# Half chunks: k transposed whole, k^T v on four tiles, the middle state on VectorE, and a table of places for every attention step

## The chip, the cores and the metric

The kernel runs on one core of one Trainium2 chip. The metric is the device time of one execution in microseconds (us), from the first instruction to the last; runs of this kernel lay between 716.03 and 719.46 us, with a median of 718.99 us. The engines are named as in the profile: PE (TensorE matmul), PEld (its weight loads), DVE (VectorE), ACT (ScalarE), POOL (GpSimd), SP (the queue that issues most DMAs). Each engine works through its own instructions in order and waits on semaphores for the others.

## The reference, cut to what matters

A gated linear attention feeds two blocks of dense layers. The change is in the attention part alone, in how it is computed for three of the four batches, and in where its steps stand.

```python
B, H, S, D = 4, 8, 768, 48
f = 1.0 / (1.0 + np.exp(-f_logit))
for t in range(S):
    state = f[:, :, t, :, None] * state + np.einsum('bhd,bhe->bhde', k[:, :, t], v[:, :, t])
    y[:, :, t] = np.einsum('bhd,bhde->bhe', q[:, :, t], state)
# then, with x = y as [B, S, 384]:
h = xt @ U @ V;  u = x + h.T;  x1 = u + relu(u @ w_ch1) @ w_ch2        # d_model 384 -> 1536 -> 384
theta = x1 @ w_theta;  y = w_tok_r @ (x1 cos) + w_tok_i @ (x1 sin);  u = x1 + y;  out = u + relu(u @ w_ch)
```

## The kernel before, in words

The sequence of a batch is cut into six chunks of 128 positions. Within a chunk the gate products p (a running product of f along the chunk) are divided out: q is multiplied by p, k by 1/p, so that scores, states and outputs become matmuls. The eight heads are packed as four pairs (index j); a pair's two heads lie on partitions 0 to 47 and 64 to 111, so that one tile row of the array (64 partitions) holds one head.

For batch 0 (`start`) a chunk is worked whole: `sc` (scores), `kt` (k transposed with four whole transposes of 112x128), `kv` (k^T v, the chunk's part of the state), `xx` (output), `xt` (output transposed). For batches 1 to 3 a chunk is worked as two halves of 64 positions, with matmuls of 64x64 tiles of the array:

- `pre_a`, `pre_s`, `pre_r` (lines 237 to 266): sigmoid on ACT, the running product as a scan on DVE, q times p on POOL, then for each pair a reciprocal on DVE, and for every second pair the product k/p on POOL.
- `kt4` (376): k transposed, as 16 matmuls of one head and one half against an identity; the results of both halves stand under each other by head, and ACT copies the bank to `ktok`.
- `sc4` (355): the scores of both halves, 16 matmuls into bank A5; `mask4` (368) multiplies them by a triangle on DVE.
- `kv4` (390): k^T v of each half, 16 matmuls (`L400`), into one bank (A3 or A4 for batches 2 and 3, B1 for batch 1). Head a of a pair takes tile row a and tile column a, so two of the four tiles are in use. ACT copies both halves' results to `kvs` (`L403`); POOL adds the old state to the first half's (`L405`: the middle state), adds that to the second half's (`L407`) and multiplies by the chunk's whole product (`L408`).
- `xx4` (412): the output, 16 matmuls of masked scores with v (`L423`), then of q with the old and the middle state (`L429`), into banks B0 and B1; ACT copies both banks to `xf`.
- `xt` (345): the output of a chunk transposed by three whole transposes of 128x128.

v is loaded by `load_v` (219): for the half chunks each half of the 128 rows is copied to both halves of the partitions, so that each head finds either half of v on its own partitions.

The attention of batch b+1 is interleaved with the first dense block of batch b, `moe1(b)` (625). `moe1` is a list of 48 steps of equal weight: `w1g` (nine matmuls of 128x384, `L639`; ACT makes hh (`L644`), DVE makes hl from the same bank (`L645`)) and `w2g` (six matmuls with hh, `L656`, three with hl, `L659`), in the order w1g 0, w1g 1, w2g 0, w1g 2, w2g 1 and so on. After the last w2g of a row of them DVE adds three accumulators to xT (`L664`). `hT` (597) is one matmul, an add to xT on DVE (`L601`), a copy on ACT and a difference on POOL; three of them stand at the start of each `moe1`.

What sets the order: `place` (147) walks the list of `moe1`'s steps and puts each timed step ahead of the `moe1` step whose middle lies at or behind its time (a share of the list). `spread` gives a list of steps evenly spaced times in an interval. Before the change the attention of batches 2 and 3 is one list (`elif b > 1`, 517) spread over 0 to 0.86 of `moe1`, after its first six steps stood in the end of the `moe1` before (`NPRE`); `opening` (kt4 and sc4 of chunk 0) comes early, and `one(c)` (446) does xt of the chunk before, kv4, kt4 and sc4 of the next chunk, and xx4, all in a row. Batch 1 has its own list (543), stretched by the knots `AKNOT`. `WPOS` holds the times of four steps for each piece of the weights of `moe1` (load, scale on ACT, join on DVE `L1001` and `L1004`, split on ACT and POOL `L164`); these stand in batch 0's attention and in `moe1(0)`.

PSUM has eight banks: A0 to A2 hold w2g's accumulators, A3 and A4 take w1g in turn, A5 the scores, B0 and B1 are shared by kt4, kv4 of batch 1, xx4, xt and hT.

## Time and profile before

| | |
|---|---|
| three runs | 718.99 us median, 716.03 to 719.46 |
| the profiled execution | 717.67 us, of which the span of its instructions is 715.9 us |
| mean granted TensorE clock | 0.991 |
| busy: PE, DVE, ACT, POOL | 692.7, 385.7, 334.4, 301.1 us (97, 54, 47, 42% of the span) |
| batch 0's attention (PE waits often) | about 0 to 67 us |
| moe1(0), moe1(1), moe1(2), with the attention of batches 1, 2, 3 | about 67 to 184, 184 to 290, 290 to 394 us |
| moe1(3), then the second dense block | about 394 to 500, 500 to 716 us |

A group of the trace gives the line, the engine, the operation, the tiles it writes and reads, the shape, and then busy time and the mean length of one instruction. Matmuls overlap in the array: a 128x384 matmul is shown some 340 ns long, but the next one starts about 173 ns later, so lengths of matmuls don't add up, and what a row of them costs is read from where it starts to where the next row starts. One `mm` call on 32-bit floats stands in the trace as two instructions, a whole transpose as one.

### The profile page before, as it was taken

The numbers are of one execution on the slowest core, as the hardware profiler recorded it, in microseconds if no ns is written. First come the engines' busy times: TensorE is split into PE (matmuls) and PEld (weight loads), VectorE is DVE, ScalarE is ACT, GpSimd is POOL, SyncE is SP. The second block draws the span as 40 slices with busy tenths as digits, with TensorE's granted clock in tenths as the row PEclk, the third lists the DMA queues.
The fourth block names the chain that finished last, engine by engine and source line by source line (L and its number), as shares of the span: only waits on it lengthen the run. The fifth ranks groups of instructions, "written<-read, shape, count | busy, mean of one in ns | idle before, by whom it ended". The sixth has DMA issues, their size and how long they took to land.

```text
span 715.9 us, 15690 instructions
## 1 busy us (share of the span) xinstructions
PE 692.7 (97%) x6601; PEld 660.9 (92%) x6601; DVE 385.7 (54%) x593; ACT 334.4 (47%) x706; POOL 301.1 (42%) x320
## 2 busy tenths in 40 slices
...
GB/s 174 247 229 180 45 105 96 64 60 102 1 56 58 57 86 82 2 57 57 58 23 1 85 117 131 118 125 89 1 1 23 33 12 12 45 12 12 33 23 71
DMA packets 20606, 49.85 MB, mean 70 GB/s; under 512 B 2576, under 2 KB 11152, under 8 KB 20528
## 3 DMA queue, kind: packets, MB, share of 16 engines
...
q8 instruction: 54, 0.88, 0.6%
q10 hardware_dynamic: 192, 0.59, 0.4%
...
## 4 chain that ended last, share of the span: by engine, by line
PE 75%; DVE 9%; ACT 6%; POOL 3%; DMA 3%; issue 3%; POOLq 0%; DVEq 0%; ACTq 0%
PE ps_A L788 17%; PE ps_A L639 17%; PE ps_A L656 11%; PE ps_A L659 5%; PE ps_B L816 5%; PE ps_B L735 4%; PE ps_B L384 2%; PE ps_A L364 2%; DMA r<-in_wtok_dram 2%; DVE f L261 2%; PE ps_A L400 2%; PE ps_B L429 1%; PE ps_B L423 1%; DVE w L1004 1%; PE ps_B L574 1%
## 5 line engine op out<-in xcount | busy, mean ns | idle before, releaser
L645 DVE SCALAR_TENSOR_TENSOR hl<-ps_A,hh 128x384 fp32r<-128x384 f32 x96 | 53.0, 553 | 160.0 <-ACT hh L644 159.5
L788 PE MATMUL ps_A<-W,zh 128*128 128x384 f32 x576 | 125.1, 338 | 0.0
L639 PE MATMUL ps_A<-uh,W 128*128 128x384 f32 x576 | 119.4, 341 | 0.9 <-ACT uh L605 0.9
L656 PE MATMUL ps_A<-hh,W 128*128 128x384 f32 x552 | 115.4, 338 | 1.6 <-DVE xT L664 0.9
L644 ACT ACTIVATE hh<-ps_A 128x384 fp32r<-128x384 f32 x96 | 46.9, 488 | 133.5 <-PE ps_A L639 132.8
L639 PEld LDWEIGHTS ps_A<-uh,W 128*128 128x128 f32 x576 | 100.9, 189 | 2.9 <-ACT uh L605 1.7
L788 PEld LDWEIGHTS ps_A<-W,zh 128*128 128x128 f32 x576 | 100.7, 188 | 0.0
L656 PEld LDWEIGHTS ps_A<-hh,W 128*128 128x128 f32 x552 | 96.3, 188 | 4.0 <-DVE xT L664 1.8
L164 POOL TENSOR_TENSOR zl<-z,zh 128x768 fp32r<-128x768 f32 x24 | 44.7, 1864 | 98.1 <-ACT zh L765 53.5
L261 DVE RECIPROCAL f<-p 112x128 f32<-112x128 f32 x96 | 85.3, 923 | 0.8
L788 PE MATMUL ps_A<-W,zl 128*128 128x384 f32 x288 | 73.3, 335 | 0.0
L659 PE MATMUL ps_A<-hl,W 128*128 128x384 f32 x276 | 66.1, 338 | 2.3 <-DVE hl L645 2.3
L639 PE MATMUL ps_A<-ul,W 128*128 128x384 f32 x288 | 66.3, 336 | 0.3 <-POOL ul L164 0.2
L164 POOL TENSOR_TENSOR ul<-xT,uh 128x384 fp32r<-128x384 f32 x45 | 45.8, 1035 | 48.9 <-ACT uh L605 32.9
L264 POOL TENSOR_TENSOR raw<-raw,f 112x256 f32<-112x256 f32 x48 | 38.1, 794 | 59.4 <-DVE f L261 59.2
L639 PEld LDWEIGHTS ps_A<-ul,W 128*128 128x128 f32 x288 | 51.5, 188 | 1.2 <-DVE ul L164 0.6
L659 PEld LDWEIGHTS ps_A<-hl,W 128*128 128x128 f32 x276 | 49.7, 189 | 2.8 <-DVE hl L645 2.7
L788 PEld LDWEIGHTS ps_A<-W,zl 128*128 128x128 f32 x288 | 52.1, 188 | 0.0
L254 POOL TENSOR_TENSOR raw<-raw,p 112x512 f32<-112x512 f32 x24 | 30.8, 1285 | 45.9 <-DVE p L250 29.6
L741 DVE SCALAR_TENSOR_TENSOR ps_B<-kk,ps_B 128x384 f32<-128x384 f32 x24 | 13.5, 562 | 60.0 <-ACT kk L740 60.0
L164 POOL TENSOR_TENSOR W<-r,W 128x384 fp32r<-128x384 f32 x24 | 27.0, 1136 | 40.1 <-ACT W L167 40.1
L574 PE MATMUL ps_B<-wz 128*128 128x384 f32 x104 | 29.5, 404 | 3.9 <-POOL wz L849 3.5
...
## 6 DMA issues: line engine op xcount, KB each, us to landing
...
```

Of the source, the lines that this page charges most:

```text
L164: eng.tensor_tensor(out=out_, in0=a, in1=b, op=ALU.subtract)
L254: nc.gpsimd.tensor_tensor(out=x, in0=x, in1=p, op=ALU.mult)
L261: nc.vector.reciprocal(out=f[:, j], in_=p[:, j])
L264: nc.gpsimd.tensor_tensor(out=x, in0=x, in1=f[:, j - 1:j + 1], op=ALU.mult)
L574: mm(out=o, lhsT=t[:, 0:128], rhs=t, start=True, stop=True)
L639: mm(out=t, lhsT=w1t(lo, fb)[:, k, 128 * fo:128 * fo + 128], rhs=x[:, k], start=(n == 0), stop=(n == 8))
L644: nc.scalar.activation(out=hh, in_=t, func=ACTF.Relu)
L645: nc.vector.scalar_tensor_tensor(out=hl, in0=t, scalar=0.0, in1=f32(hh), op0=ALU.max, op1=ALU.subtract)
L656: mm(out=st["acc"][k], lhsT=w2t(lo, fb)[:, fo, 128 * k:128 * k + 128], rhs=hh, start=(first_of(f) and lo == 0), stop=False)
L659: mm(out=st["acc"][k], lhsT=w2t(0, fb)[:, fo, 128 * k:128 * k + 128], rhs=hl, start=False, stop=last_of(f))
L788: mm(out=t, lhsT=z[:, i, 128 * k:128 * k + 128], rhs=w[:, S * i + HT * th:S * i + HT * th + HT], start=(s == 0 and n == 0), stop=(s == NCH ...
L816: mm(out=t, lhsT=w[:, k, 128 * m:128 * m + 128], rhs=x[:, k], start=(n == 0), stop=(n == 8))
```

## The change

k of the half chunks is transposed as in batch 0, by `kt` with four whole transposes, and `kt4` is gone. `ktok` now holds the 128 positions on the partitions, a half on each tile row, and both heads beside each other, so `kv4` takes the half as the tile row and the head as the tile column: four tiles, with a bank for each half (B0 and B1; A3 and A4 are left to w1g). v lies as it was loaded in `vt[:, 0]` and with its halves swapped in `vt[:, 1]`, by three DMAs where there were two; `xx4` picks the one or the other by head. The middle state is made by one DVE add that reads the bank (`L399` of the changed kernel), in place of an ACT copy and the POOL add; ACT copies the second half's result alone. `wst` (the state as batch 0 uses it) becomes a part of the tile that holds the states. `kt` moves to its own place ahead of the chunk, with two buffers for `ktok`, in bank B0 for batches 2 and 3 (B1 for batch 1), and `xt` to its own place behind the chunk, in B1. The table `A2` gives each of the ten steps of each chunk of batches 2 and 3 a time of its own; a row is a chunk, and the columns are pre_a, pre_s, four pre_r, kt, mask4, run_ (kv4, sc4 of the next chunk, xx4, the next loads), xt; times of 1 and more are in the second `moe1`. Of the tables `WPOS`, `LN`, `AKNOT`, `APOS` and `H1` the numbers change a little.

```diff
-NPRE = 6
...
 WPOS = (
     (0.1862, 0.1897, 0.3792, 0.4046),
...
-    (1.0258, 1.1848, 1.22, 1.258),
-    (0.9521, 1.2359, 1.2388, 1.3545),
...
+    (1.0417, 1.1879, 1.2226, 1.2611),
+    (0.9806, 1.2189, 1.2421, 1.3578),
...
+A2 = (
+    (0.8611, 0.8711, 0.8911, 0.8992, 0.9211, 0.9372, 1.0131, 1.0303, 1.1011, 1.1303),
+    (0.9414, 1.0014, 1.0032, 1.0283, 1.0431, 1.0664, 1.0794, 1.1318, 1.2384, 1.2798),
...
-    kvs = [ap_.tile([PR, 2, NP, D], F32, name=f"kvs{i}") for i in range(2)]
+    kvt = ap_.tile([PR, 2, 2, NP, D], F32, name="kvt")
+    kvs = [kvt[:, i] for i in range(2)]
+    wst = kvt[:, :, 0]
...
-    wst = ap_.tile([PR, NP, 2, D], F32, name="wst")
...
             vt = vbuf[(g + 1) % 2]
+            nc.sync.dma_start(out=vt[:, 0], in_=src)
             for o in (0, 64):
-                nc.sync.dma_start(out=vt[o:o + 64], in_=src.rearrange("(i s) f -> s i f", i=2))
+                nc.sync.dma_start(out=vt[64 - o:128 - o, 1], in_=src[o:o + 64])
...
         def kt(c):
...
-            t = ps("A4", [128, NP, PR])
+            t = ps("A4" if start else "B1" if b == 1 else "B0", [128, NP, PR])
             for j in range(NP):
                 nc.tensor.transpose(t[:, j], r[0:PR, 1, j], ident[0:PR, 0:PR])
-            k = ap_.tile([128, NP, PR], F32, tag="kt", bufs=1, name="ktok")
+            k = ap_.tile([128, NP, PR], F32, tag="kt", bufs=2, name="ktok")
...
-                w = wst.rearrange("p j a e -> p j (a e)")
                 for j in range(NP):
                     for o in halves:
-                        mm(out=t[o, 96 * j:96 * j + 96], lhsT=r[0:PR, 0, j, o], rhs=w[:, j],
+                        mm(out=t[o, 96 * j:96 * j + 96].rearrange("p (a e) -> p a e", a=2), lhsT=r[0:PR, 0, j, o], rhs=wst[:, :, j],
...
-            t = ps("A1" if start else "B0", [128, NK, CH])
+            t = ps("A1" if start else "B0" if b == 1 else "B1", [128, NK, CH])
...
-        def kt4(c):
...
         def kv4(c):
 
             g = b * NCH + c
             n = 2 if c + 1 < NCH else 1
-            t = ps("B1" if b == 1 else f"A{4 - st['f'] % 2}", [PR, 2, NP, D])
+            t = [ps(x, [PR, NP, D]) for x in ("B0", "B1")[0:n]]
             k, vt = st["k", g], st["v", g]
-            for i in range(n):
-                for j in range(NP):
+            for j in range(NP):
+                for i in range(n):
+                    s = slice(64 * i, 64 * i + 64)
                     for o, e in ((0, 64), (64, PR)):
                         h = 2 * j + o // 64
-                        mm(out=t[o:e, i, j], lhsT=k[o:o + 64, i, j, 0:e - o], rhs=vt[o:o + 64, i, D * h:D * h + D],
-                           start=(i + j == 0), stop=(i == n - 1 and j == NP - 1), skip_group_check=True)
+                        mm(out=t[i][o:e, j], lhsT=k[s, j, o:e], rhs=vt[s, 0, D * h:D * h + D],
+                           start=(j == 0), stop=(j == NP - 1), skip_group_check=True)
             new, old = kvs[g % 2], kvs[(g + 1) % 2]
-            nc.scalar.activation(out=new[:, 0:n], in_=t[:, 0:n], func=ACTF.Copy)
             if c:
-                nc.gpsimd.tensor_tensor(out=new[:, 0], in0=new[:, 0], in1=old[:, 1], op=ALU.add)
+                nc.vector.tensor_tensor(out=new[:, 0], in0=t[0], in1=old[:, 1], op=ALU.add)
+            else:
+                nc.scalar.activation(out=new[:, 0], in_=t[0], func=ACTF.Copy)
             if n > 1:
+                nc.scalar.activation(out=new[:, 1], in_=t[1], func=ACTF.Copy)
...
-                           rhs=vt[o:o + 64, i, D * h:D * h + D], start=(j == 0), stop=False, skip_group_check=True)
+                           rhs=vt[o:o + 64, i ^ a, D * h:D * h + D], start=(j == 0), stop=False, skip_group_check=True)
...
-        def opening():
-            kt4(0)
-            sc4(0)
...
         def one(c):
 
-            if c:
-                xt(c - 1)
             kv4(c)
             if c + 1 < NCH:
-                kt4(c + 1)
                 sc4(c + 1)
             xx4(c)
...
-                add(0, kt4, c)
+                add(0, kt, c)
...
+            def kt_(c):
+                kt(c)
+                if c == 0:
+                    sc4(0)
+
+            def run_(c):
+                one(c)
+                nxt_load(c)
+
+            fs = [pre_a, pre_s] + [lambda c, j=j: pre_r(c, j) for j in range(NP)] + [kt_, mask4, run_, xt]
+            for c, at in enumerate(A2):
+                for f, x in zip(fs, at):
+                    L.append((x, lambda f=f, c=c: f(c)))
...
+        att = {b: attention(b) for b in range(2, B)}
+        early = lambda b: [(x, f) for x, f in att[b] if x < 1.0] if 1 < b < B else []
+        late = lambda b: [(x - 1.0, f) for x, f in att[b] if x >= 1.0] if b > 1 else []
...
-                     (0.945, 0.985, prelude_h(b + 1, 0)), (0.86, 0.94, ahead[:NPRE])]
+                     (0.945, 0.985, prelude_h(b + 1, 0))]
...
-            else:
-                lanes.append((0.0, 0.86, att))
-            del ahead[:NPRE]
-            place(moe1(b), [x for lane in lanes for x in spread(*lane)] + (timed[1] if b == 0 else []))
+            place(moe1(b), [x for lane in lanes for x in spread(*lane)] + late(b + 1) + early(b + 2)
+                  + (timed[1] if b == 0 else []))
```

On PE, chunk 3 of batch 2: before, the end of kv4 (one bank, `ps_A_3070`, tile pairs of 64 and 48 columns), then kt4 and sc4 of the next chunk, then xx4:

```order
L400 MATMUL ps_A_3070<-vt_86,ktok 64x48
L400 MATMUL ps_A_3070<-vt_86,ktok 48x48
L384 MATMUL ps_B_3091<-ident,raw_78 64x64 x16
L364 MATMUL ps_A_3110<-raw_78 64x64 x16
L423 MATMUL ps_B_3127<-vt_86,m 64x48
L423 MATMUL ps_B_3128<-vt_86,m 64x48
```

and now, where 2903 and 2904 are the two halves' banks (B0 and B1), and 2942 and 2943 those of xx4 (B0 and B1 again):

```order
L395 MATMUL ps_B_2903<-vt_84,ktok 64x48
L395 MATMUL ps_B_2903<-vt_84,ktok 48x48
L395 MATMUL ps_B_2904<-vt_84,ktok 64x48
L395 MATMUL ps_B_2904<-vt_84,ktok 48x48
L372 MATMUL ps_A_2925<-raw_78 64x64 x16
L420 MATMUL ps_B_2942<-vt_84,m 64x48
L420 MATMUL ps_B_2943<-vt_84,m 64x48
```

The transposition is gone from between kv4 and xx4, kv4 alternates between two banks, and xx4 writes the same two banks next. On DVE the same chunk's new add stands here, behind the three adds to xT that follow the last w2g of a row:

```order
L624 SCALAR_TENSOR_TENSOR hl<-ps_A_2870,hh 128x384
L643 TENSOR_TENSOR xT_1170<-ps_A_2294,xT_1170 128x384
L643 TENSOR_TENSOR xT_1170<-ps_A_2295,xT_1170 128x384
L643 TENSOR_TENSOR xT_1170<-ps_A_2296,xT_1170 128x384
L399 TENSOR_TENSOR kvt<-ps_B_2903,kvt 112x192
L259 SCALAR_TENSOR_TENSOR p<-f,first_74 112x512
```

and before there was nothing between those adds and the scan of the next chunk:

```order
L645 SCALAR_TENSOR_TENSOR hl<-ps_A_2947,hh 128x384
L664 TENSOR_TENSOR xT_1179<-ps_A_2359,xT_1179 128x384
L664 TENSOR_TENSOR xT_1179<-ps_A_2360,xT_1179 128x384
L664 TENSOR_TENSOR xT_1179<-ps_A_2361,xT_1179 128x384
L250 SCALAR_TENSOR_TENSOR p<-f,first_73 112x512
```

So DVE has one more instruction there, for which PE's xx4 waits. On DVE, the start of moe1(1) before (xT_318 is the last add of the batch that ends, xT_1179 belongs to the three hT, p to the scan of chunk 1 of batch 2, f to its reciprocals, m to the mask of chunk 0):

```order
L664 TENSOR_TENSOR xT_318<-ps_A_2161,xT_318 128x384
L645 SCALAR_TENSOR_TENSOR hl<-ps_A_2313,hh 128x384
L601 TENSOR_TENSOR xT_1179<-ps_B_2327,xT_1179 128x384
L250 SCALAR_TENSOR_TENSOR p<-f,first_74 112x512
L645 SCALAR_TENSOR_TENSOR hl<-ps_A_2337,hh 128x384
L371 TENSOR_TENSOR m<-ps_A_2296,tri 128x512
L261 RECIPROCAL f<-p 112x128
L601 TENSOR_TENSOR xT_1179<-ps_B_2354,xT_1179 128x384
L261 RECIPROCAL f<-p 112x128
L645 SCALAR_TENSOR_TENSOR hl<-ps_A_2373,hh 128x384
L601 TENSOR_TENSOR xT_1179<-ps_B_2387,xT_1179 128x384
L261 RECIPROCAL f<-p 112x128 x2
```

and now:

```order
L643 TENSOR_TENSOR xT_316<-ps_A_2099,xT_316 128x384
L259 SCALAR_TENSOR_TENSOR p<-f,first_74 112x512
L270 RECIPROCAL f<-p 112x128
L624 SCALAR_TENSOR_TENSOR hl<-ps_A_2220,hh 128x384
L580 TENSOR_TENSOR xT_1170<-ps_B_2258,xT_1170 128x384
L270 RECIPROCAL f<-p 112x128
L379 TENSOR_TENSOR m<-ps_A_2241,tri 128x512
L624 SCALAR_TENSOR_TENSOR hl<-ps_A_2269,hh 128x384
L580 TENSOR_TENSOR xT_1170<-ps_B_2288,xT_1170 128x384
L270 RECIPROCAL f<-p 112x128 x2
L580 TENSOR_TENSOR xT_1170<-ps_B_2308,xT_1170 128x384
```

The scan and the reciprocals of chunk 1 moved ahead of work on which PE's hT wait; in PE's row kt of chunk 1 now stands behind the third w1g. On DVE, two joins of weights (`w_877`, then `w_810`) in moe1(0) before:

```order
L645 SCALAR_TENSOR_TENSOR hl<-ps_A_1081,hh 128x384
L1001 SCALAR_TENSOR_TENSOR w_877<-w_877 128x768
L1004 SCALAR_TENSOR_TENSOR w_877<-w_877 128x768
L261 RECIPROCAL f<-p 112x128
L1001 SCALAR_TENSOR_TENSOR w_810<-w_810 128x768
L1004 SCALAR_TENSOR_TENSOR w_810<-w_810 128x768
L645 SCALAR_TENSOR_TENSOR hl<-ps_A_1148,hh 128x384
L645 SCALAR_TENSOR_TENSOR hl<-ps_A_1232,hh 128x384
```

and now (`w_903`, then `w_853`):

```order
L624 SCALAR_TENSOR_TENSOR hl<-ps_A_1071,hh 128x384
L979 SCALAR_TENSOR_TENSOR w_903<-w_903 128x768
L982 SCALAR_TENSOR_TENSOR w_903<-w_903 128x768
L270 RECIPROCAL f<-p 112x128
L624 SCALAR_TENSOR_TENSOR hl<-ps_A_1136,hh 128x384
L979 SCALAR_TENSOR_TENSOR w_853<-w_853 128x768
L982 SCALAR_TENSOR_TENSOR w_853<-w_853 128x768
L624 SCALAR_TENSOR_TENSOR hl<-ps_A_1211,hh 128x384
```

One hl moved ahead of the second join.

## Rows read from the trace of the kernel before

**Rows 1.** The chain of work that ended last (start, us, what): one w1g.

```profile
193.36 1.56 PE ps_A L639 x9
```

**Rows 2.** Stretches: length; busy PE, PEld, DVE, ACT, POOL (instructions); clock; DMA; GB/s.

```profile
100.00:110.00 10.00, 7.67 (x61) 7.04 (x61) 8.67 (x12) 2.77 (x6) 3.72 (x5) 0.83 0.99 244
...
180.00:280.00 100.00, 99.56 (x1365) 96.46 (x1364) 46.08 (x68) 35.01 (x82) 36.49 (x49) 1.00 0.29 61
```

**Rows 3.** Groups by shape on PE: the old transposition, masked scores, whole transposes, batch-0 output.

```profile
L384 PE MATMUL ps_B<-ident,raw 48*64 48x64 f32 x576 | 21.6, 221 | 0.3 <-POOL raw L264 0.3
...
L423 PE MATMUL ps_B<-vt,m 64*64 64x48 f32 x576 | 12.3, 222 | 0.1
...
L317 PE MATMUL ps_B<-vt,m 128*64 128x48 f32 x192 | 7.2, 233 | 0.0
...
L296 PE MATMUL ps_A<-ident,raw 112*128 112x112 f32 x24 | 3.6, 275 | 0.0
```

**Rows 4.** PE in order of time (start, length, what), a chunk of batch 2.

```profile
196.41 1.07 PE L400 MATMUL ps_A<-vt,ktok 64*64 64x48 f32 x31
...
197.37 1.05 PE L384 MATMUL ps_B<-ident,raw 48*64 48x64 f32 x30
...
198.32 1.04 PE L364 MATMUL ps_A<-raw 48*64 48x64 f32 x30
...
199.20 0.67 PE L423 MATMUL ps_B<-vt,m 64*64 64x48 f32 x30
199.70 0.63 PE L429 MATMUL ps_B<-kvs,raw 48*64 48x48 f32 x16
```

**Rows 5.** PE in order of time, whole transposes in batch 0's attention.

```profile
22.77 0.55 PE L296 MATMUL ps_A<-ident,raw 112*128 112x112 f32 x4
23.16 0.54 PE L352 MATMUL ps_A<-ident,xf 128*128 128x128 f32 x3
23.45 0.77 PE L574 MATMUL ps_B<-wz 128*128 128x384 f32 x3
```

**Rows 6.** Groups on POOL: k/p, and the add of the old state.

```profile
L264 POOL TENSOR_TENSOR raw<-raw,f 112x256 f32<-112x256 f32 x48 | 38.1, 794 | 59.4 <-DVE f L261 59.2
...
L405 POOL TENSOR_TENSOR kvs<-kvs,kvs 112x192 f32<-112x192 f32 x15 | 8.9, 593 | 38.0 <-ACT kvs L403 38.0
```

**Rows 7.** Waits of PE: what waited for whom, us in total, times, longest.

```profile
PE ps_B L429 <- POOL kvs L405: 0.8, 2, 0.4
```

**Rows 8.** DVE in order of time, the start of moe1(1).

```profile
182.17 1.49 DVE L664 TENSOR_TENSOR xT<-ps_A,xT 128x384 f32<-128x384 f32 x3 [0.66 <-PE ps_A L659]
...
187.30 0.55 DVE L601 TENSOR_TENSOR xT<-ps_B,xT 128x384 f32<-128x384 f32 x1
187.76 1.21 DVE L250 TENSOR_TENSOR_SCAN p<-f,first 112x512 f32<-112x512 f32 x1
188.90 0.53 DVE L645 SCALAR_TENSOR_TENSOR hl<-ps_A,hh 128x384 fp32r<-128x384 f32 x1
189.34 0.68 DVE L371 TENSOR_TENSOR m<-ps_A,tri 128x512 f32<-128x512 f32 x1
189.94 0.94 DVE L261 RECIPROCAL f<-p 112x128 f32<-112x128 f32 x1
190.80 0.49 DVE L601 TENSOR_TENSOR xT<-ps_B,xT 128x384 f32<-128x384 f32 x1
```

**Rows 9.** The weights' join on DVE: its line's lengths (min/median/max ns).

```profile
L1004 DVE SCALAR_TENSOR_TENSOR w<-w x6: 959/960/6834, 45.8 to 95.5; 128x768 int32<-128x768 int32 x6
```

**Rows 10.** All engines in order of time, moe1(0), 95 to 103 us.

```profile
95.50 6.83 DVE L1004 SCALAR_TENSOR_TENSOR w<-w 128x768 int32<-128x768 int32 x1
...
96.01 3.68 POOL L164 TENSOR_TENSOR W<-xT,W 128x768 fp32r<-128x768 f32 x2
...
99.65 1.87 POOL L164 TENSOR_TENSOR W<-w,W 128x768 fp32r<-128x768 f32 x1
...
102.85 1.33 PE L659 MATMUL ps_A<-hl,W 128*128 128x384 f32 x3 [2.33 <-DVE hl L645]
```

More of the change, by code (lines that the diff above doesn't have):

```diff
@@ L72 @@
     (0.1862, 0.1897, 0.3792, 0.4046),
[L73 to L91 removed]
+    (0.1795, 0.3112, 0.4572, 0.559),
+    (0.1661, 0.2816, 0.7593, 0.7701),
+    (0.2003, 0.3559, 0.7797, 0.8951),
+    (0.4487, 0.6487, 0.7903, 0.8884),
+    (0.3124, 0.4627, 0.8453, 0.9487),
+    (0.5959, 0.7377, 0.9379, 1.0221),
+    (0.5615, 0.6918, 1.0533, 1.0836),
+    (0.5284, 1.1474, 1.1668, 1.2493),
+    (0.794, 1.0598, 1.1556, 1.2466),
+    (1.0417, 1.1879, 1.2226, 1.2611),
+    (0.9806, 1.2189, 1.2421, 1.3578),
+    (1.0937, 1.3034, 1.409, 1.4223),
+    (1.2508, 1.492, 1.5527, 1.5827),
+    (1.2564, 1.6316, 1.6579, 1.7489),
+)
+LN = (0.0549, 0.1387)
+AKNOT = (0.0298, 0.3138, 0.5099, 0.6663, 0.9061)
+APOS = (0.7516, 0.8647, 0.9379, 0.9596, 0.9433, 1.0876)
+A2 = (
[6 rows of a table added]
+)
+H1 = (0, 0.0804)
 P_MIN = 2.0 ** -60
@@ L342, in blocks @@
             for q, o in ((0, 0), (1, 64)):
-                nc.scalar.activation(out=wst[o:o + D, :, q], in_=kvs[(b * NCH + c) % 2][o:o + D, 1], func=ACTF.Copy)
+                nc.scalar.activation(out=wst[o:o + D, q], in_=kvs[(b * NCH + c) % 2][o:o + D, 1], func=ACTF.Copy)
         def xt(c):
@@ L374, in mask4 @@
             st["m", g] = m
-        def kt4(c):
-            g = b * NCH + c
-            r = rawof(g)
-            t = ps("B1", [128, 2, NP, 64])
-            for j in range(NP):
-                for i in range(2):
-                    for o in (0, 64):
-                        mm(out=t[o:o + 64, i, j], lhsT=r[o:o + D, 1, j, 64 * i:64 * i + 64],
-                           rhs=ident[o:o + D, o:o + 64], start=(i + j == 0), stop=(i + j == NP), skip_group_check=True)
-            k = ap_.tile([128, 2, NP, 64], F32, tag="kt", bufs=1, name="ktok")
-            nc.scalar.activation(out=k, in_=t, func=ACTF.Copy)
-            st["k", g] = k
         def kv4(c):
@@ L516, in attention @@
             warm(KEEP[8])
-        elif b > 1:
-            add(200, pre_a, 0)
-            add(1000, pre_s, 0)
-            for j in range(NP):
-                add(1000, pre_r, 0, j)
-            add(100, pre_a, 1)
-            add(1000, opening)
-            add(1000, pre_s, 1)
-            add(0, mask4, 0)
-            for j in range(NP):
-                add(1000, pre_r, 1, j)
-            for c in range(NCH):
-                n2 = c + 2 < NCH
-                if n2:
-                    add(1500, pre_a, c + 2)
-                add(3000, one, c)
-                if n2:
-                    add(1000, pre_s, c + 2)
-                if c + 1 < NCH:
-                    add(0, mask4, c + 1)
-                if n2:
-                    for j in range(NP):
-                        add(1000, pre_r, c + 2, j)
-                add(0, nxt_load, c)
-            add(400, xt, NCH - 1)
-        else:
+        elif b == 1:
             add(200, pre_a, 0)
@@ L568, in attention @@
             add(400, xt, NCH - 1)
+        else:
+            def kt_(c):
[9 more added lines that the diff above has]
+                    L.append((x, lambda f=f, c=c: f(c)))
         return L
```

26 lines of the change are left out of this document (3 added, 23 removed), and 4 rows, old and new, of the table A2.

## The prediction

> **What bounds the kernel now.** I read the stretches first. From 180 to 280 us, which is one whole moe1 with a batch of attention beside it, PE is busy for 99.56 of 100 us at the full clock, DVE for 46.08, ACT and POOL for about 36 [rows 2]. Second, the chain of waits: in that part it is PE's own rows, one w1g of 1.56 us after the other [rows 1]. So from 110 to 394 us the time is the sum of what PE has to do. What the attention takes off PE's row comes off the end, one for one, as long as no other engine makes PE wait instead. Third, PE's waits: of the half-chunk steps only the second half of xx4 waits for anything of weight, 0.8 us for POOL's add of the old state [rows 7]. Before 110 us it is different: at 102.85 PE waits 2.33 us for a hl that stands on DVE behind a join of weights that took 6.83 us [rows 10], and the stretch from 100 to 110 us has PE busy for 7.67 of 10 us at a granted clock of 0.83 [rows 2].
>
> **The change part by part: k transposed whole.** kt4 starts at 197.37 and the next row, sc4, at 198.32: 0.95 us for 32 instructions [rows 4]. Four whole transposes start at 22.77 and what follows starts at 23.16: 0.39 us; three of 128x128 take 0.29 [rows 5], which is the same price each. Two tile rows work side by side in kt4, yet each loads new weights every time, and that is dearer than four passes through the whole array. Saved: 0.56 us in each of 18 chunks, **10.1 us**. Were the transposes as dear as their busy time (3.6 us for 24, so 0.60 for four [rows 3]), it would be 0.35 x 18 = 6.3 us. On ACT the copy out is of 448 columns instead of 512: nothing on the path.
>
> **k^T v on four tiles.** kv4 starts at 196.41, the next row at 197.37: 0.96 us for 32 instructions on two of four tiles [rows 4]. The nearest row with four tiles is the masked-score part of xx4, L423: the same 64 rows, 64 columns and 48 moving columns, 32 instructions, 0.50 us from 199.20 to 199.70 [rows 4]. I take that row: 0.46 us saved in each of 15 chunks, **6.9 us**. The last chunk of a batch has one half, thus one tile row and two columns: 16 instructions as before, nothing saved. The lower end is nothing at all: L423 changes the tile row with each call, the new kv4 walks both columns of a row first.
> The row that bears on this is batch 0's output, L317: both columns, all rows, 7.2 us for 192 instructions, 37 ns each with the tail [rows 3], where kv4's two rows give 0.96 us / 32 = 30 ns. Columns overlap nearly as well as rows do. The Trainium skill, page TensorE: Matmul & The Clock Gate, Part 3, says that a weight load overlaps running matmuls only when the row group differs. By that rule half of the new kv4's loads would wait, the saving would be near 0 and the time 6.9 us longer; this trace speaks against it with the 37 ns.
>
> **The middle state on VectorE.** An ACT copy of 384 columns becomes one of 192, POOL loses 15 adds of 0.59 us [rows 6], DVE gains 15 of 112x192 from a bank. No row shows that; DVE's 128x384 add takes 0.55 us [rows 8], so half of it, 0.27, and 0.55 are the ends, and I take 0.35. That is 5 us on an engine with half its time free: nothing by itself. Its place matters, since kv4 now lies in the banks that xx4 writes next: before, xx4's first half could run while the state was made; now xx4 stands still until DVE and ACT have emptied both banks. Behind kv4's end PE has sc4 of the next chunk, 0.88 us (198.32 to 199.20 [rows 4]); drain and add want about 0.6, so in most chunks there is no wait. Three of the six chunks (counted from 0) of batches 2 and 3 differ. In chunk 3 the add stands behind three adds to xT: they last 1.49 us [rows 8], with the add 1.75 after the last w2g, against 0.50 + 0.88 = 1.38 on PE: 0.4 us. In chunk 2 a hl stands just ahead: 0.3. In chunk 5 there is no sc4 between: 0.5. Together 1.2 us a batch, **+2.4**. The old wait of 0.8 goes: **-0.8**. Batch 1 has a moe1 step between kv4 and xx4 in nearly all chunks: nothing.
>
> **The table of places.** Most steps stand where their inputs are several us old. The start of moe1(1) and of moe1(2) is tighter. Before, kt4 and sc4 of chunk 0 filled PE while DVE did the three adds to xT; now w1g comes first, and DVE has the scan and a reciprocal ahead of the first hl. By DVE's pitch from one start to the next (scan 1.14, hl 0.44, mask 0.60, reciprocal 0.86, add 0.46; the three adds 1.40 [rows 8]), counted from the end of the last w2g: scan done at 2.54, reciprocal 3.40, hl 3.84, first hT's add 4.30, reciprocal 5.16, mask 5.76, hl 6.20, second hT's add 6.66, two reciprocals 8.38, then POOL's product 0.79 [rows 6]: 9.2. PE: w1g 1.56 [rows 1], kt 0.39, sc4 0.88, hT 0.17, w1g, hT, w2g reach 6.29, where the third hT needs the bank that is free at 6.66; then w1g, and kt of chunk 1 at 8.39 wants k that is ready at 9.2. 0.4 + 0.8 = 1.2 us, twice: **+2.4**. Ends: 0, and 4 if overlaps are worse.
>
> **Joins of weights.** In moe1(0) the hl that PE waited for now stands ahead of the second join. The wait cost 2.33 us, and at clock 0.83 a further 0.17 x 10 = 1.7 [rows 2, 10]: the mean of 10 us that began with an idle PE and then had some time at 1.2 GHz. The join will still be held while POOL splits weights (96.01 to 101.52 [rows 10]); the hl behind it is now the next one, which PE needs a w1g and a w2g later, 3.1 us. That covers the wait nearly, not surely: of 4.0 us I take **-2.5**; ends 0 and -4.0.
>
> **The rest at nothing.** v takes three DMAs instead of two; it is asked for two chunks ahead. The state of batch 0 is read as two runs of 48 columns instead of one of 96, 80 instructions: at the worst one more pass of 37 ns each, 3 us, and no row shows any price. xt in a place and a bank of its own is the same three transposes.
>
> **Sum** against the profiled execution, 717.67: -10.1 - 6.9 + 2.4 - 0.8 + 2.4 - 2.5 = -15.5, so 702.2. The median of the runs is 1.3 above that execution: **703.5 us**.
>
> **The rivals.** First, the tiles don't overlap in the new order, the second column of a tile row waiting for the first: kv4 stays at 0.96, and 703.5 + 6.9 = 710.4. For it: the order of tiles differs from L423's; against it: L317. Second, the join's wait stays: +2.5, and of the 1.5 us or so that PE saves ahead of it (two kt, one kv4) nothing arrives: 707.5. For it: a join that took 6.83 us has a median of 0.96 [rows 9], and POOL's three splits still follow each other. The Trainium skill, page SBUF — State Buffer, Who interferes with whom, says that a VectorE instruction with two inputs in SBUF is shut out while GpSimd reads SBUF; the row agrees, and by that rule the join would be held in its new place as in its old one. Third, the other side: PE waits in every chunk, because the bank that kv4 left is emptied by an engine with a queue. If two reciprocals (1.7 us by pitch) stood ahead of the add in each of the 10 chunks of batches 2 and 3 that have it, that is 17 us, with 3 us at each start of a moe1 and one more spell at 1.2 GHz of 1.7, and nothing of the join's wait won: -17.0 - 0.8 + 17 + 6 + 1.7 = +6.9, so 725.9 from the median of 719.0. It decides from some 20 us of new waits on; against it: in DVE's row a reciprocal stands directly ahead of none of those adds. Fourth, the transposition doesn't get cheaper in this place: 703.5 + 10.1 = 713.6; four whole transposes stand in PE's row, so that only their price could do it.
>
> **How the numbers follow.** Forecast 0.66, tiles 0.12, join 0.13, transposition 0.04, waits everywhere 0.05. Range: downwards no new waits (-4.8) and the whole join won (-1.5) would be 697.2, I put 697.5; upwards the first rival, 710.4, put at 711. What can be told from no change is 0.5%, 3.6 us: all but the third and a part of the fourth lie below 715.4, so faster 0.90, same 0.06, slower 0.04.
>
> **What would show it.** kt as four rows that cost 0.4 us to the next row; kv4 at 0.5 us against 0.96; a DVE add of 0.35 us; PE idle between sc4 and xx4 in chunks 2, 3 and 5 alone; PE idle of about 1 us in the first 10 us of moe1(1) and moe1(2), ended by an add to xT and by POOL; no wait of 2.3 us and no 0.83 around 100 us. I am wrong if kv4's row is near 0.9 us, if PE's waits for DVE or ACT come to more than 8 us between 110 and 394, or if the second block, which is not touched, changes.

## The result, and the profile after

| | before | after |
|---|---|---|
| median of four runs each | 719.23 us | 707.43 us (704.89 to 709.53) |
| ratio of the two, 95% interval | | 0.9845 (0.9802 to 0.9887) |
| profiled execution, its span | 717.67, 715.9 us | 707.19, 705.4 us |

The change takes off 11.8 us by the medians and 10.5 by the profiled executions; 15.5 were forecast. Lines have moved: w1g is `L618`, w2g `L635` and `L638`, kt `L305`, sc4 `L372`, kv4 `L395`, the DVE add `L399`, xx4 `L420` and `L426`. The first w1g of moe1(0), (1), (2) and (3), in the timeline of PE, before and after:

```profile
67.05 0.44 PE L639 MATMUL ps_A<-uh,W 128*128 128x384 f32 x1 [0.85 <-ACT uh L605]
184.43 0.45 PE L639 MATMUL ps_A<-uh,W 128*128 128x384 f32 x1
290.33 0.45 PE L639 MATMUL ps_A<-uh,W 128*128 128x384 f32 x1
393.86 0.33 PE L639 MATMUL ps_A<-uh,W 128*128 128x384 f32 x1
```

```profile
69.74 0.44 PE L618 MATMUL ps_A<-uh,W 128*128 128x384 f32 x1 [0.85 <-ACT uh L584]
178.53 0.33 PE L618 MATMUL ps_A<-uh,W 128*128 128x384 f32 x1
280.59 0.33 PE L618 MATMUL ps_A<-uh,W 128*128 128x384 f32 x1
382.55 0.33 PE L618 MATMUL ps_A<-uh,W 128*128 128x384 f32 x1
```

So the three moe1 with attention beside them, 326.8 us before, take 312.8: **-14.0**. Ahead of them batch 0's attention, whose code hardly changed, takes 2.7 us more, and behind them the lead stays about the same: the last addition to the output starts 11.64 us earlier (DVE, before and after), and only the last transfer took 1.1 longer.

```profile
710.06 0.56 DVE L822 SCALAR_TENSOR_TENSOR o<-ps_B,xT 128x384 f32<-128x384 f32 x1 [1.01 <-PE ps_B L816]
```

```profile
698.42 0.56 DVE L801 SCALAR_TENSOR_TENSOR o<-ps_B,xT 128x384 f32<-128x384 f32 x1 [1.01 <-PE ps_B L795]
```

The new steps after, in PE's timeline (the second number is a group's length; the price of a step is read from its start to the start of the next row's group):

```profile
180.57 0.55 PE L305 MATMUL ps_B<-ident,raw 112*128 112x112 f32 x4
181.05 1.15 PE L372 MATMUL ps_A<-raw 48*64 48x64 f32 x32
...
184.15 1.20 PE L635 MATMUL ps_A<-hh,W 128*128 128x384 f32 x6
185.19 0.68 PE L638 MATMUL ps_A<-hl,W 128*128 128x384 f32 x3
...
203.57 0.62 PE L395 MATMUL ps_B<-vt,ktok 64*64 64x48 f32 x30
...
204.06 1.05 PE L372 MATMUL ps_A<-raw 48*64 48x64 f32 x30
...
205.00 0.58 PE L420 MATMUL ps_B<-vt,m 64*64 64x48 f32 x28
...
215.83 0.55 PE L305 MATMUL ps_B<-ident,raw 112*128 112x112 f32 x4
216.15 1.30 PE L618 MATMUL ps_A<-uh,W 128*128 128x384 f32 x6
217.29 0.52 PE L618 MATMUL ps_A<-ul,W 128*128 128x384 f32 x2
```

kv4 takes 0.49 us (0.96 in [rows 4]), kt 0.32 ahead of a w1g and 0.48 ahead of sc4 (kt4 0.95). The neighbours of kt pay too: the six multiplications of 128x384 behind it take 1.14, six at 184.15 take 1.04. PE stays the bound of the middle stretch, as in [rows 2]:

```profile
180.00:280.00 100.00, 98.84 (x1218) 94.52 (x1218) 50.82 (x75) 35.41 (x87) 34.54 (x45) 1.00 0.30 61
```

Its waits, first from 110 to 178.5 us, then in moe1(1) (waiting line, what it waited for, us in total, times, longest):

```profile
PE ps_B L420 <- DVE kvt L399: 2.3, 1, 2.3
PE ps_B L305 <- POOL raw L273: 0.8, 1, 0.8
```

```profile
PE ps_B L420 <- DVE kvt L399: 0.5, 1, 0.5
PE ps_B L305 <- POOL raw L273: 0.3, 1, 0.3
PE ps_A L618 <- POOL ul L171: 0.2, 1, 0.2
```

The first is new and large. In chunk 1 of batch 1 xx4 waits for a middle state that VectorE makes late; the queue of VectorE shows why:

```profile
96.50 6.83 DVE L979 SCALAR_TENSOR_TENSOR w<-w 128x768 int32<-128x768 int32 x1
103.37 0.96 DVE L982 SCALAR_TENSOR_TENSOR w<-w 128x768 int32<-128x768 int32 x1
...
107.70 0.94 DVE L270 RECIPROCAL f<-p 112x128 f32<-112x128 f32 x1
108.55 1.42 DVE L643 TENSOR_TENSOR xT<-ps_A,xT 128x384 f32<-128x384 f32 x3
109.89 0.35 DVE L399 TENSOR_TENSOR kvt<-ps_B,kvt 112x192 f32<-112x192 f32 x1
```

The second join is held as long as before ([rows 10]): there it was its second instruction, here it is its first (`L979`), and the second takes 0.96. The hl that PE waited for now stands ahead of it, and the next hl, behind it, costs PE 0.4 us where there were 2.33. But what gathers behind the join delays the addition, and xx4 starts at 110.29, 2.28 us late.

Then there is the clock. From 51 to 58 us PE ran at 0.50 of its clock (1.2 GHz), before at a mean of 0.76 (columns as in [rows 2]):

```profile
51.00:58.00 7.00, 6.88 (x66) 4.96 (x66) 5.50 (x6) 2.84 (x7) 4.08 (x4) 0.76 0.77 199
```

```profile
51.00:58.00 7.00, 6.94 (x73) 5.56 (x71) 6.51 (x8) 1.88 (x6) 4.03 (x4) 0.50 0.59 174
```

Is this the change's doing? Most of the experiments repeat that code unaltered, and it comes and goes among them.

### The profile page after: what moved, and what is told of

The parts are those of the page before. It is cut to its first block, busy times and chain, and to the rows that moved or that the text cites. A ratio compares the mean times of both kernels' runs of the same rounds, so it can differ in the third digit from the quotient of the medians.

```text
span 705.4 us, 14710 instructions
## 1 busy us (share of the span) xinstructions
PE 678.6 (96%) x6097; PEld 644.5 (91%) x6097; DVE 390.4 (55%) x608; ACT 329.7 (47%) x706; POOL 294.9 (42%) x305
## 4 chain that ended last, share of the span: by engine, by line
PE 73%; DVE 7%; ACT 6%; DMA 5%; issue 4%; POOL 3%; SPq 1%; POOLq 0%; ACTq 0%; DVEq 0%
PE ps_A L767 18%; PE ps_A L618 15%; PE ps_A L635 10%; PE ps_B L795 5%; PE ps_A L638 5%; PE ps_B L714 4%; PE ps_A L372 2%; DMA r<-in_wtok_dram 2%; PE ps_B L553 2%; DMA w<-in_w_dram 2%; PE ps_B L395 1%; PE ps_B L420 1%; DVE w L979 1%; PE ps_B L426 1%; PE ps_B L305 1%
## 5 line engine op out<-in xcount | busy, mean ns | idle before, releaser
L618 PE MATMUL ps_A<-uh,W 128*128 128x384 f32 x576 | 119.0, 340 | 0.9 <-ACT uh L584 0.9
L635 PE MATMUL ps_A<-hh,W 128*128 128x384 f32 x552 | 116.9, 341 | 1.4 <-DVE xT L643 0.9
L618 PEld LDWEIGHTS ps_A<-uh,W 128*128 128x128 f32 x576 | 99.8, 188 | 2.7 <-ACT uh L584 1.7
L635 PEld LDWEIGHTS ps_A<-hh,W 128*128 128x128 f32 x552 | 95.5, 188 | 3.8 <-DVE xT L643 1.8
L618 PE MATMUL ps_A<-ul,W 128*128 128x384 f32 x288 | 66.4, 336 | 0.6 <-POOL ul L171 0.6
L638 PE MATMUL ps_A<-hl,W 128*128 128x384 f32 x276 | 65.6, 335 | 0.4 <-DVE hl L624 0.4
L618 PEld LDWEIGHTS ps_A<-ul,W 128*128 128x128 f32 x288 | 51.4, 188 | 1.7 <-POOL ul L171 1.6
L638 PEld LDWEIGHTS ps_A<-hl,W 128*128 128x128 f32 x276 | 49.4, 188 | 0.8 <-DVE hl L624 0.7
L263 POOL TENSOR_TENSOR raw<-raw,p 112x512 f32<-112x512 f32 x24 | 31.6, 1317 | 42.7 <-DVE p L259 18.2
L171 POOL TENSOR_TENSOR xlo<-xf,xhi 128x384 fp32r<-128x384 f32 x18 | 18.2, 1013 | 41.1 <-ACT xhi L436 41.1
```

The source lines that it names most:

```text
L171: eng.tensor_tensor(out=out_, in0=a, in1=b, op=ALU.subtract)
L263: nc.gpsimd.tensor_tensor(out=x, in0=x, in1=p, op=ALU.mult)
L618: mm(out=t, lhsT=w1t(lo, fb)[:, k, 128 * fo:128 * fo + 128], rhs=x[:, k], start=(n == 0), stop=(n == 8))
L635: mm(out=st["acc"][k], lhsT=w2t(lo, fb)[:, fo, 128 * k:128 * k + 128], rhs=hh, start=(first_of(f) and lo == 0), stop=False)
L638: mm(out=st["acc"][k], lhsT=w2t(0, fb)[:, fo, 128 * k:128 * k + 128], rhs=hl, start=False, stop=last_of(f))
```

## The experiments

Lengths in us from the first w1g of one moe1 to that of the next; "start" is the first w1g of moe1(0). Before, kt4 and sc4 of the next batch's first chunk (2.0 us) stood in the moe1 ahead, so that before's moe1(2) lacks them and its moe1(0) has them twice. Each ratio is to the runs of before that were timed beside that kernel. A "spell" is a stretch in which PE was granted 1.2 GHz.

| kernel | start | moe1(0) | moe1(1) | moe1(2) | median of runs | ratio to before |
|---|---|---|---|---|---|---|
| before | 67.05 | 117.4 | 105.9 | 103.5 | | |
| after | 69.74 | 108.8 | 102.1 | 102.0 | 707.4 | 0.9845 |
| e1_kt_tiles | 68.44 | 112.1 | 103.8 | 103.8 | 712.7 | 0.9936 |
| e2_kv_by_row | 69.20 | 109.8 | 102.7 | 102.7 | 708.8 | 0.9884 |
| e3_kv_rows_alternate | 65.56 | 108.8 | 102.1 | 102.0 | 704.7 | 0.9823 |
| e4_state_pool | 65.53 | 108.6 | 103.1 | 102.8 | 706.8 | 0.9855 |
| e5_join_later | 68.03 | 111.7 | 102.1 | 102.0 | 707.2 | 0.9823 |
| e6_old_tables | 69.19 | 109.0 | 103.1 | 102.9 | 708.8 | 0.9845 |
| e7_kt_in_run | 69.83 | 111.8 | 101.8 | 101.8 | 708.1 | 0.983 |
| e8_scale_later | 68.24 | 108.7 | 102.1 | 102.0 | 706.1 | 0.9819 |
| e9_state_first | 67.06 | 107.8 | 102.1 | 102.0 | 704.3 | 0.9822 |
| e10_fill | 66.03 | 111.8 | 102.1 | 102.0 | 705.5 | 0.9828 |
| e11_two_tiles | 68.48 | 113.1 | 106.2 | 105.8 | 719.5 | 1.0028 |
| e12_both | 66.54 | 107.8 | 102.0 | 102.0 | 703.3 | 0.9799 |

**Both tile steps undone.**

```diff
-                nc.tensor.transpose(t[:, j], r[0:PR, 1, j], ident[0:PR, 0:PR])
+                            mm(out=t[o:o + 64, i, j], lhsT=r[o:o + D, 1, j, 64 * i:64 * i + 64], rhs=ident[o:o + D, o:o + 64], ...)
-                        mm(out=t[i][o:e, j], lhsT=k[s, j, o:e], rhs=vt[s, 0, D * h:D * h + D], ...)
+                        mm(out=t[i][o:e, j], lhsT=k[o:o + 64, i, j, 0:e - o], rhs=vt[o:o + 64, i ^ a, D * h:D * h + D], ...)
```

> The changed kernel with both tile steps as before the change: k by 32 multiplications with the identity on two of four tiles (in batches 2 and 3 between kv4 and sc4, where a whole transposition costs no more than at its own place), kv4 on two of four tiles; v, banks, middle state on VectorE, places of all other steps as changed. Theory A, the tile steps are the whole gain in moe1: kt 0.46 to 0.95 and kv4 0.46 to 0.90 us, 6 x 0.49 + 5 x 0.45 = 5.2 us more for moe1(1) and for moe1(2), 107.2 each against 102.0, and 4 to 5 more for moe1(0); 722 in all. Rival B, part of the gain is the own places and the state on VectorE: 104.5 to 106 each, 716 to 719.

The whole gain is gone: 719.5, ratio 1.0028 (1.0001 to 1.0055). The three moe1 take 325.1 us, 12.3 more than after. A had said 722 and 107.2 a moe1, B 716 to 719 and 104.5 to 106: moe1(1) and moe1(2) lie at B's upper end, but in the median no gain is left for the rest of the change. In the timeline of this kernel kv4 (`L403`), kt4 (`L313`) and sc4 (`L381`):

```profile
206.59 1.07 PE L403 MATMUL ps_B<-vt,ktok 64*64 64x48 f32 x31
...
207.56 1.05 PE L313 MATMUL ps_A<-ident,raw 48*64 48x64 f32 x30
...
208.50 1.04 PE L381 MATMUL ps_A<-raw 48*64 48x64 f32 x30
```

That is 1.91 us for the two steps. The same place with the new forms is the next run.

**Whole transposition in the old place.**

```diff
             kv4(c)
             if c + 1 < NCH:
+                kt(c + 1)
                 sc4(c + 1)
...
             def kt_(c):
-                kt(c)
                 if c == 0:
+                    kt(0)
                     sc4(0)
```

> The changed kernel, but in batches 2 and 3 k of the next chunk is transposed (whole, four instructions) between kv4 and sc4, where kt4 stood before, and not at a place of its own beside a w1g; it uses a bank of the w1g ring. Theory A, a change between steps on whole-array and on 64x64 tiles costs PE some 0.26 us each time (w2g ahead of kv4 takes 0.79 and not 0.52): the step in the middle pays two, 10 x (0.3 to 0.6) = 3 to 6 us more over both moe1, 103.5 to 105 each against 102.0. Rival B, the place costs nothing: 102.0 within 0.5 each, the transposes 0.4 to 0.46 wherever they stand.

Rival B: 101.8 each, the own place wins nothing (the 111.8 of moe1(0) come from a spell at the lower clock, below). But the row shows a price that the forecast lacked, and rival B too (0.4 to 0.46 wherever they stand):

```profile
205.45 0.68 PE L395 MATMUL ps_B<-vt,ktok 64*64 64x48 f32 x32
206.06 0.60 PE L305 MATMUL ps_A<-ident,raw 112*128 112x112 f32 x4
206.59 1.08 PE L372 MATMUL ps_A<-raw 48*64 48x64 f32 x29
```

kv4 takes 0.61 here, 0.49 where another tile step follows it; the transposes take 0.53, 0.39 between two whole-array steps ([rows 5]). Each change between tile work and whole-array work costs 0.12 to 0.14. So e11's pair costs 1.91 us and this one 1.14, 0.77 less a chunk and not the 1.02 that the forecast added up. In its own place kt is cheap and its neighbours are dearer. This is moe1(1) in the four kernels, added up from the start of each of PE's instructions to the start of the next, with the waits apart (us):

| step | before | e11 | e7 | after |
|---|---|---|---|---|
| kt4 or kt | 5.9 | 5.9 | 3.2 | 2.5 |
| kv4 | 5.3 | 5.3 | 3.7 | 3.0 |
| sc4 | 5.4 | 5.4 | 5.7 | 5.9 |
| w1g and w2g | 76.1 | 77.3 | 77.2 | 77.9 |
| xt | 2.4 | 1.5 | 1.5 | 1.5 |
| xx4 | 7.0 | 6.8 | 6.5 | 6.6 |
| hT and the rest | 3.4 | 3.4 | 3.4 | 3.5 |
| PE's waits | 0.4 | 0.7 | 0.7 | 1.2 |

From e11 to after the two steps' own rows save 5.7, and moe1(1) gets only 4.2 shorter: sc4, w1g and w2g and the waits take 1.6 of it back.

**k on four tiles, kv4 in other orders.** e1, then e2, then e3:

```diff
-                nc.tensor.transpose(t[:, j], r[0:PR, 1, j], ident[0:PR, 0:PR])
+                    for i in range(2):
+                        for o in (0, 64):
+                            mm(out=t[o // 64][64 * i:64 * i + 64, j], lhsT=r[o:o + D, 1, j, 64 * i:64 * i + 64], rhs=ident[o:o + D, o:o + 64], ...)
```

```diff
-            for j in range(NP):
-                for i in range(n):
+            for i in range(n):
+                for j in range(NP):
```

```diff
-                for i in range(n):
-                    for o, e in ((0, 64), (64, PR)):
+                for o, e in ((0, 64), (64, PR)):
+                    for i in range(n):
```

> The changed kernel, but k is transposed again by 32 small multiplications with the identity in each chunk of batches 1 to 3, this time on all four tiles (before: two of four), into two banks, with two copies out on ScalarE. Theory A, a tile can take a new weight only every 55 to 60 ns, so what counts is how many tiles work in turn: the step costs 0.45 to 0.50 us, as much as the four whole transposes of the changed kernel (0.46), and the time stays within 1.5 us of 707.4. Theory B, small multiplications that each load a weight are dear in themselves and the whole transposes are what saved: 0.9 us a step, 18 x 0.45 = 8 us more, about 715.

> The changed kernel, but kv4 does all 16 multiplications of the first half (tile row 0) and then the 16 of the second, so that two tiles work at any time instead of four; nothing else differs. Theory A (a tile takes a new weight every 55 to 60 ns): 0.42 us a step becomes about 0.9, 15 x 0.48 = 7 us more, 714.5. Rival B, weight loads overlap between columns as freely as between rows and only the number of instructions counts: 0.42 as now, 707.4. Rival C, a load overlaps only with multiplications in the other tile row: each load waits for the multiplication ahead, at least 32 x 55 ns = 1.8 us a step, 15 x 1.35 = 20 us more, 727 or later.

> The changed kernel, but kv4 changes the tile row with each instruction, where the changed kernel does both columns of a row first; the four tiles still take turns. Theory A (only the number of tiles in turn counts): 0.42 us a step as now, 707.4 within 1 us. Rival C (a load overlaps only with multiplications in the other tile row): half of the loads wait now and none would here, so the step gets at least 0.1 us shorter, 15 x 0.1 = 1.5 us or more off.

e1 lies between A and B. The step takes 0.63 us where four whole transposes take 0.32 (at 215.83 above), and moe1(1) and moe1(2) are 1.8 us longer, 0.3 a chunk. In moe1(0) it also met a spell, and the step, which now needs both banks, waited there 2.3 us for ACT to empty one; so its median is no measure of the tiles alone.

```profile
218.51 0.69 PE L314 MATMUL ps_B<-ident,raw 48*64 48x64 f32 x32
219.14 1.31 PE L628 MATMUL ps_A<-uh,W 128*128 128x384 f32 x6
```

In e2 kv4 takes 0.72 (two rows, kv4 and sc4), between A's 0.9 and B's 0.42; of the 0.23 a part comes back in the next step (sc4 takes 5.7 us in moe1(1), 5.9 after), so that a moe1 loses 0.6 to 1.0. e3 equals after in every stretch: the order among four tiles doesn't matter.

```profile
204.27 0.77 PE L395 MATMUL ps_B<-vt,ktok 64*64 64x48 f32 x27
...
204.99 0.92 PE L372 MATMUL ps_A<-raw 48*64 48x64 f32 x25
```

Per instruction kv4 takes 15 ns on four tiles, 23 on the two of a row, 30 on two in a diagonal. The more tiles take turns the better, but the number alone doesn't set it: theory A's fixed time for a tile falls with e2.

**Who makes the middle state, and the join.** e4, e5 and e6 (which takes `WPOS`, `LN`, `AKNOT`, `APOS` and `H1` from the kernel before):

```diff
-                nc.vector.tensor_tensor(out=new[:, 0], in0=t[0], in1=old[:, 1], op=ALU.add)
+            nc.scalar.activation(out=new[:, 0], in_=t[0], func=ACTF.Copy)
...
+                nc.gpsimd.tensor_tensor(out=new[:, 0], in0=new[:, 0], in1=old[:, 1], op=ALU.add)
```

```diff
-    (0.9806, 1.2189, 1.2421, 1.3578),
+    (0.9806, 1.2189, 1.305, 1.3578),
```

```diff
-LN = (0.0549, 0.1387)
...
-H1 = (0, 0.0804)
+LN = (0.027, 0.1291)
...
+H1 = (0.0, 0.09)
```

> The changed kernel, but the middle state is made as before: ScalarE copies both halves out of their banks, GpSimd adds the old state; no addition on VectorE. Theory A, xx4 of chunk 1 of batch 1 waits 2.3 us because the addition on VectorE stands behind what a held join of weights left queued: that wait goes; the next hl, in the same queue, then holds a w2g for about 1 us, so some 1.3 us are won there. In batches 2 and 3 the banks are emptied by ScalarE, whose two copies of about 0.3 us come one after the other: chunk 3's wait of 0.2 goes, the last chunk's stays at about 0.5 and xx4's second half waits some tenths for GpSimd. Sum -2 to +0.5: 705.4 to 708. Rival B, the wait is kv4's own place, any engine that empties the banks is late: the 2.3 us stay and GpSimd's addition adds 0.4 to 0.8 in each batch: 708 to 709.5.

> The changed kernel with one number of the table of weights altered: the second of the two joins near 96 us in moe1(0), held for 6.83 us while GpSimd splits weights, stands behind the next hl and the scan, some 6 us later. Length of moe1(0) from its first w1g to the first of moe1(1): 108.8 us in the changed kernel (69.74 to 178.53). Theory A, PE's waits there (0.4 for hl, 2.3 for the middle state on VectorE) both come from what the held join left queued on VectorE: behind the splits the join takes about 1 us, both waits go, moe1(0) takes 106.1 to 107, and the time falls by about 2. Rival B, VectorE simply has too much to do from 95 to 112 us, or the join is held wherever it stands: moe1(0) 108 to 109, the wait stands at another step, the time as before within 0.8.

> The changed kernel with the places of the weights' steps, of the preludes and of batch 1's steps as in the kernel before (the four tables that the change re-tuned); the half-chunk steps stay as changed. Theory A, the second join stands ahead of a hl again and PE waits as before, 2.3 us and a spell at the lower clock: moe1(0) takes 2 to 4 us more than the 108.8 of the changed kernel. Rival B, the new places won nothing, since the wait only moved to the middle state: moe1(0) within 1 us of 108.8. Batches 2 and 3 from 178 us on are untouched: 102.0 each.

Three times the wait only changed its place. The largest wait of PE between 66 and 183 us in e4, e5 and e6:

```profile
PE ps_B L426 <- POOL kvt L402: 1.3, 1, 1.3
```

```profile
PE ps_B L420 <- DVE kvt L399: 3.4, 1, 3.4
```

```profile
PE ps_A L638 <- DVE hl L624: 2.5, 1, 2.5
```

In e4 moe1(0) gains 0.2 and the other two lose 0.8 to 1.0 each, since xx4's second half waits for GpSimd again (0.6 of it is a listed wait): in these two VectorE is the better place for the state, though the medians of e4 and after don't tell them apart. e5 lets hl through, and VectorE idles for 4.28 us ahead of it and has the join in its way later: theory A falls. In e6 the old wait for hl is back and moe1(0) is as long as after (109.0): what the new tables won at hl they lost at the middle state. The expectation that moe1(1) and moe1(2) stay at 102.0 failed: `H1`, the one table that reaches them, costs 1.0 us in each, and kt waits 1.8 us for GpSimd in moe1(1), 0.3 after.

**VectorE's queue in chunk 1 of batch 1.**

```diff
+                rs = [[], [], [0], [1, 2, 3]] if c == 1 else [[0], [1], [2], [3]]
...
-                    add(1000, pre_r, c + 1, 0)
-                    add(1000, pre_r, c + 1, 1)
+                    add(1000, rr, rs[0])
+                    add(1000, rr, rs[1])
                 add(500, kv4, c)
```

`rr` runs the reciprocals of its list; of the four, one stands right behind the addition and three behind the next hl.

> The changed kernel, but in chunk 1 of batch 1 the four reciprocals stand behind the middle state's addition on VectorE instead of two of them ahead of it; no other engine's order changes. Theory A, xx4 waits there because of what is queued ahead of the addition (2.3 us, in the profiles with this code always within 0.1): the two reciprocals are 1.7 us of that, the wait falls to about 0.6 and moe1(0), which takes 108.6 to 109.0 in profiles without a spell at the lower clock there, takes 107.0 to 107.4. Rival B, the next thing in VectorE's queue (hl, or the reciprocals that kt of chunk 2 needs) then comes late by as much: 108.5 or more.

```profile
PE ps_B L420 <- DVE kvt L399: 0.7, 1, 0.7
```

The wait falls from 2.3 to 0.7 and moe1(0) by 1.0, not 1.6: between A and B, for kt of chunk 2 then takes 0.5 us longer: it stops in its middle for the product that GpSimd makes from the later reciprocals. With the join in its place, what is queued ahead of the addition is the cause.

**The clock.** e8, then e10; e12 is e9 and e10 together.

```diff
-    (0.5959, 0.7377, 0.9379, 1.0221),
+    (0.5959, 0.86, 0.9379, 1.0221),
```

```diff
+                    warm(8 if c == 4 else 0)
                     add(900, kv, c)
...
-                warm(KEEP[6])
+                warm(6 if c == 3 else KEEP[6])
```

> The changed kernel with one number altered: in batch 0 the two ScalarE steps on the piece of weights that lands at 45.2 us stand behind the copies of xf and k that PE waits for, some 8 us later. Theory A, batch 0 is as long as it is because ScalarE waits for that transfer with xf queued behind it, PE stands still for 2.0 us and then runs at the lower clock for a time that differs from execution to execution: the first w1g of moe1(0) starts by 65.5 or earlier (69.74, 69.20, 68.44 in three profiles that had a spell at the lower clock, 65.56 and 65.53 in two that had none), the median falls by 1 to 3 us and the runs lie closer together. Rival B, PE then waits for k's copy or for GpSimd in the same place: nothing changes, spells at the lower clock come as before.

> The changed kernel with 14 more idle multiplications on PE in batch 0, six ahead of the transposes that wait for xf and eight ahead of the multiplication that waits for k's copy, some 1.1 and 1.5 us: as long as PE stands there in the profiles without a spell at the lower clock (1.0 and 1.6). Theory A, it is this idle time of PE, between 44 and 51 us, after which the granted clock falls to 1.2 GHz for 4 to 10 us: with PE busy the clock stays at 1.00 from 44 to 66 us, the first w1g of moe1(0) starts at 65.5 in each run and not at up to 69.7; the median falls by 1.5 to 3 us and the runs stand closer together. Rival B, the spell does not come from these waits: spells as before, and where the fillers are longer than the wait they cost up to 1 us, 707.4 to 708.5.

> The changed kernel with the edits of the two runs before taken together: the 14 idle multiplications in batch 0, and the middle state's addition ahead of the reciprocals in chunk 1 of batch 1. Theory A, a spell at the lower clock comes only where PE stood for some us just before, which is at 44 to 51 us in batch 0 and at 105 to 110 us in moe1(0), by chance in some executions and not in others: with PE busy at the first place and the wait at the second cut from 2.3 to 0.7 us, neither comes; the first w1g starts at 66.0, moe1(0) takes 107.8, moe1(1) and moe1(2) 102.0 each, the mean granted clock is 0.995 or more, and the median is 702 to 704 with little scatter (707.4 for the changed kernel, 704.3 and 705.5 for one edit each). Rival B, spells come in some executions wherever PE stands still for a moment, for one place closed another opens: 704 to 706.5, runs up to 710 as before.

e8: rival B, PE then stands 2.6 us for k's copy, and the spell comes; its median, 706.1, lies within the scatter of after. The code of batch 0 up to 58 us is the same in after, e1 to e5, e7, e9 and e11; its start of moe1(0) lies at 65.5 in the two profiles at full clock (e3, e4) and between 67.06 and 69.83 in the others. So the 2.7 us that batch 0 lost lie within what chance does; whether the change made spells more frequent is not shown. e3 and e10 from 51 to 58 us, then e10 from 104 to 116:

```profile
51.00:58.00 7.00, 6.88 (x108) 5.11 (x110) 6.97 (x8) 4.10 (x8) 5.79 (x5) 1.00 0.71 199
```

```profile
51.00:58.00 7.00, 6.88 (x107) 5.05 (x104) 6.97 (x8) 4.13 (x8) 5.21 (x5) 1.00 0.75 197
104.00:110.00 6.00, 3.74 (x70) 3.33 (x70) 4.66 (x9) 1.79 (x5) 3.77 (x5) 0.71 0.11 21
110.00:116.00 6.00, 6.00 (x55) 5.66 (x54) 0.93 (x2) 2.14 (x6) 1.56 (x2) 0.72 0.74 147
```

e10 keeps the clock in batch 0, but falls at the second place, behind the 2.3 us for the middle state: 3 us in moe1(0), as in e5 and e7. After itself, with the same wait, was spared in its profile. e12 takes both away, and in all six of its runs the mean granted clock is 0.995 to 0.998 (0.984 to 0.994 in after's four): 702.8 to 705.2 us, median 703.3, ratio 0.9799 (0.9772 to 0.9827), theory A. It beats both kernels, after by about 4 us of medians, though the two were timed beside different runs of before and their intervals overlap. Of the 44 runs of the nine kernels named above, which keep that code of batch 0, 6 reach 0.995. So removing PE's idle time removes most of the spells; why one follows in one execution and not in the next stays open.

## Why the prediction was right, and where its sizes failed

- **PE is the sum, and the tiles are the gain: right.** e11 returns to 719.5 with these two steps alone.
- **kv4 -6.9: right.** 0.49 us a step; over the three moe1 its rows fall from 16.4 to 9.6 us, 6.7 saved. The rival of tiles that don't overlap (710.4) is out: e3 is indifferent to the order, and e2, on two tiles of one row, takes 0.72. The rule of the Trainium skill (TensorE: Matmul & The Clock Gate, Part 3), that a weight load overlaps only multiplications of another row group, doesn't hold in these rows: by it e2 should be dearer than the old diagonal pair (0.96), and it is cheaper.
- **kt -10.1: right for its own rows.** Over the three moe1 they fall from 18.2 to 7.9 us, 10.3 saved.
- **The steps beside them, put at nothing: the term that failed.** The prediction priced kt and xt in places of their own without their neighbours. In moe1(1) w1g and w2g cost 1.8 us more than before and sc4 0.5 more, xt and xx4 1.3 less: 1.0 lost. That, with kt's waits, is why undoing the two steps costs 12.3 us and not 17.0.
- **New waits at xx4, +2.4 and -0.8: half as large.** 0.5 us is listed in each of moe1(1) and moe1(2), for chunk 5; in chunks 2 and 3 no wait is listed, and xx4 starts about 0.1 later behind sc4 than in chunk 1. The old wait is gone, and the DVE add takes 0.35. What failed is "batch 1: nothing": 2.3 us there, the addition being behind the join's backlog.
- **Starts of moe1, +2.4: too high.** kt and w1g wait 0.5 us in all in moe1(1), as in moe1(2).
- **The join, -2.5: failed.** The second rival was the truth in this place, by a way that it did not name: hl got through, and the wait went to the middle state. e6 shows the sum, 109.0 against 108.8. Before's profile also had a spell behind the old wait, which after's was spared: its hl row took 1.13 us and the next six multiplications 1.92, where 0.52 and 1.04 are usual, 1.5 us together (the hl row is in [rows 10]; before's next two rows follow).

```profile
103.98 2.10 PE L639 MATMUL ps_A<-uh,W 128*128 128x384 f32 x6
105.90 0.70 PE L639 MATMUL ps_A<-ul,W 128*128 128x384 f32 x3
```

- **At nothing:** the strided reading of the state in batch 0 is free: its matmuls (`L319`) cost 4.2 us from start to start, as before.
- **Together**, over the three moe1 of the two profiles: the tile rows -17.0, as forecast; PE's waits +3.0 (3.9 to 6.9), where the forecast's terms make +1.7; the other rows about +1.5, forecast 0; the spell -1.5, forecast -0.2. That is the -14.0. What lies between it and the 11.8 of the medians is mostly batch 0's clock, 2.7 us in this profile. What lies behind the three moe1 takes 0.3 less of 316 us: it hardly changed, as forecast.
- **Luck.** The median, 707.43, falls on the second rival's 707.5, but the spells of batch 0 have a large part in that, which the rival does not name. With no spell in its profile e3, whose moe1 are after's, takes 703.1, near the forecast of 703.5, although that started from a profile of before with spells in it. At a like clock the gain stands as well: the ten runs of before with a mean granted clock of 0.996 or more took 714.2 to 715.6 us, 11 to 12.5 more.
